# Block attention and a two-layer network on one core: the order list of the first two chunks written anew, and the intermediate tiles of the second layer moved to the front of on-chip memory

## The chip, the cores and the metric

The kernel runs on one core of a Trainium2 chip. Five engines work side by side, each through its own queue of instructions in program order: PE (matrix products), DVE (VectorE), ACT (ScalarE), POOL (GpSimd) and SP, which here issues the transfers (DMA). The metric is device time in microseconds (us): the median of the runs of the whole kernel, lower is better.

## The reference

```python
B, H, S, D = 4, 8, 768, 64;  block, window = 32, 16
k_sum = k.reshape(B, H, nb, block, D).max(axis=3)
v_sum = v.reshape(B, H, nb, block, D).mean(axis=3)
scores_l = where(|i - j| < window, scale * q @ k.T, -1e9)
scores_s = scale * q @ k_sum.T + log(block)
a = softmax(concat([scores_l, scores_s]))          # over the last axis
attn = a @ concat([v, v_sum])
x = attn.transpose(0, 2, 1, 3).reshape(3072, 512)
h = maximum(x @ w_in, 0)                           # w_in 512 x 2048
out = (h * h) @ w_out                              # w_out 2048 x 512
```

## The kernel before

Attention is worked in 24 tiles of 128 query rows (tile g). Two tiles make a chunk c of 256 rows of x, so there are twelve chunks. The network's weights are cut into 16 blocks f of 128 hidden units; block f holds both its part of w_in and its part of w_out. Each operand of a network product is split into a high and a low part, and each product is three matmuls (high by high, low weight by high, high by low): `ffn1` (line 403) is 12 matmuls of 256 columns for one f, `ffn2` (line 447) is 6 of 512 columns. xh and xl are the two parts of x (lines 387 and 390), gh and gl the two parts of the squared hidden values, w_sb the two parts of the weights. All weights stay on the chip once they are converted.

The weights come as 8-byte numbers into a room of 8192 bytes per partition (w_raw) and are turned into their parts by six steps: sign (ACT, line 239), round (ACT, line 246, or DVE, line 244), shift (DVE, line 250), add (POOL, line 255), copy of the high part into a second room (line 128) and subtraction that gives the low part (line 264, DVE or POOL). There are 18 rooms, so a late weight can only be loaded when an earlier w_raw room has been given back by its subtraction.

The loop over chunks 2 to 11 is regular: eight slots of two weight blocks for each chunk, with the attention of the next two tiles placed among them by `period`. Before it, the first two chunks, eight attention tiles and the conversion of all weights are worked in an order written out by hand, the string START. Each engine keeps that order for its own instructions. A token is a step, its indices, after them the engine (a, v, p for ACT, DVE, POOL) and after "=" the PSUM bank:

- `L:` a transfer on SP's queue (kv and kw: keys or values, transposed; q, k, v, x; w for weights; mask for the constants consts_sb); KS/KT and VT block maxima of keys and block sums of values (DVE, lines 190, 195); S scores; TT mask and row maximum of one head (DVE, line 307); SB and EX subtraction and exponential of four heads; NR, N the inverse of the sum and its product; T, TC turning by PE and copy out (line 128); TU turning by DVE (line 359); O outputs of a tile (line 373); XH, XL the parts of x.
- HI, LO, SH, AD, CA, SU the six steps of the conversion of weight f (`.0`, `.1`, `.2` mean whole, w_in half, w_out half).
- `F1.u.j`, `F2.u.j` first and second layer of unit u, half j. A unit is a pair of weight blocks for one chunk: units 0, 1 are pairs 0, 1 of chunk 0; 2 to 5 pairs 0 to 3 of chunk 1; 6 to 11 pairs 2 to 7 of chunk 0; 12 to 15 pairs 4 to 7 of chunk 1. RE, SQ, MU, GL make gh and gl from F1's result; EV moves a finished output out; Z are products with zeros while PE has nothing else.

The units named in ON_POOL have their gl made by POOL (line 654), the others by DVE (line 425):

```python
        elif op == "GL":
            gh, gl = flat(gh_sb, i % 2), flat(gl_sb, i % 2)
            if i in ON_POOL:
                nc.gpsimd.tensor_sub(out=gl, in0=r_of[i], in1=gh.bitcast(F32))
            else:
                low_square(gl, ph_of[i], gh)
```

Of the kernel before, what the change touches and what calls it, by code (L numbers as in the profile page):

```python
# [40 lines left out]


START = """
Z18 L:kv0 L:kv1 KS0 KS1 L:kv2 L:q0 L:kv3 L:q1 KS2 S0.0=01 Z3 S1.0=23 L:mask KS3 S1.1=23 PK4v L:w0.1 TT0.3 TT0.0 TT0.1
TT0.2 TT1.2 L:q2 XT PK5a SB0.0p S0.1=45 Z1 L:w1.1 TT1.3 L:w2.2 L:q4 TT1.0 LO0.1a L:q3 S2.0=01 S2.1=01 Z5 TT1.1 TT1.6
EX0.0 TT0.4 SB1.0p TT0.7 L:x1 HI0.1 TT0.6 TT0.5 EX1.0 NR0.0 SB0.1p TT1.5 EX0.1 HI1.1 L:x0 N0.0p TT1.7 HI2.2 T0.0=4 Z2
TT1.4 NR1.0 S3.1=52 NR0.1 SB1.1p TT2.0 SH1.1 S3.0=52 N0.1v TC0.0a TT2.3 TT2.1 N1.0p EX1.1 NR1.1 T0.1=3 L:x3 SH0.1
LO1.1a LO2.2a T1.0=4 TT2.7 TC0.1a CA0.1a CA1.1a TT2.6 SV0 L:x2 N1.1p TT2.5 TT2.2 SB2.0p TT3.3 TT3.0 T1.1=3 Z8 TT2.4
TT3.2 L:w2.1 TC1.0a TT3.1 L:k4 SB2.1v L:w1.2 L:w3.1 EX2.0 TT3.7 TC1.1a NR2.0 EX2.1 SV1 L:w4 SB3.0p TT3.4 N2.0p EX3.0
TT3.6 S4.1=01 TT3.5 HI2.1 L:q6 VC0.0a SB3.1p VC0.1a NR2.1 NR3.0 VC0.2v AD0.1 L:w0.2 VC1.3v VC1.2v L:k5 S4.0=01 T2.0=4  # L50
VC0.3a VC1.0v L:q5 N2.1p O0=3 EX3.1 VC1.1a NR3.1 N3.0p VX2a XH0 TC2.0v O1=2 T2.1=5 TT4.1 LO2.1a XL0 XH1 TC2.1v N3.1p
TT4.3 XL1 SU0.1p TT4.4 T3.0=4 TT4.5 L:w3.2 HI3.1 TT4.6 T3.1=3 TT4.7 LO1.2a O2=5 VX3a XH2 AD1.1 TC3.0a HI0.2 SU1.1v
F1.0.0=2 SH2.1 SH3.1 F1.0.1 TC3.1v TT4.2 S5.1=43 TT4.0 CA2.1a SH0.2 AD2.1 SU2.1v LO3.1a LO0.2a XL2 AD3.1 CA3.1a O3=0
SH2.2 HI1.2 L:w6 SU3.1v L:w7 S5.0=43 SH1.2 L:w5 XH3 LO3.2a TT5.0 RE0a XL3 F1.1.0=1 AD2.2 F1.1.1 SQ0 F1.3.0=5 MU0
F1.2.0=0 RE1v AD1.2 F1.2.1 AD0.2 F1.3.1 GL0v HI4 TT5.7 HI3.2 L:w11 CA0.2v L:w10 SH3.2 SU0.2v CA1.2a LO4a SH4 CA2.2a
SU1.2v CA3.2a CA4a SU2.2v SQ1 RE2v F2.0.0 LO5a L:w13 AD3.2 F2.0.1 MU1 SQ2 AD4 HI5 GL1v RE3a F2.1.0 MU2 SU3.2v HI6 L:w9
L:w8 F2.1.1 SU4v SH5 AD5 GL2v L:w14 EV0.1v EV0.0v LO6a SH6 CA5a SQ3 TT5.2 LO7v MU3 AD6 HI7 F1.6.0=2 F1.4.0=1 CA6a HI8
F2.2.0 GL3v LO9a F2.2.1 F2.3.0 LO8a F2.3.1 SU5v SU6v TT5.6 SH8 L:kw2 L:q7 SH7 F1.4.1 HI9 RE4v VT2 F1.6.1 TT5.4 CA7a
AD7 SQ4 E4.2 L:kw1 CA8a F1.5.0=0 E4.6 E5.2 MU4 AD8 L:k6 E4.4 F1.7.0=5 GL4v E4.7 TT5.1 TT5.3 F2.4.0 TT5.5 SU7v SU8v
LO10v F2.4.1 SH9 KT2 AD9 E4.3 F1.5.1 RE6v F1.12.0=1 E5.0 F1.7.1 LO11a CA9a SU9v RE5a HI10 L:w12 MU5 SQ5 HI12 HI11 SH10  # L60
GL5v MU6 HI13 F1.8.0=3 LO12a RE7v F1.8.1 SH12 AD10 CA10v SQ6 SU10v F1.12.1 E4.0 F2.5.0 E5.7 F2.5.1 F1.9.0=4 SH11 AD11
LO13a MU7 L:v4 F1.13.0=0 GL6v EV1.0a EV1.1a SQ7 VT1 CA12a GL7v RE8a AD12 E4.5 SU12v CA11a F2.6.0 SH13 CA13a E5.3 E4.1
E5.6 F2.6.1 SQ8 SU11v F2.7.0 NR4.1 L:kw3 F2.7.1 AD13 E5.5 HI14 LO14a F1.9.1 MU8 KT1 F1.10.0=2 SH14 NR4.0 L:k7 CA14a
SU13v GL8p RE9a E5.4 AD14 NR5.1 KT3 MU9 SQ9 F2.8.0 GL9v F1.14.0=5 SU14p L:w15 F2.8.1 N4.0v VT3 N4.1v E5.1 F1.10.1 HI15
RE10a SH15 F1.14.1 LO15a F1.11.0=3 MU10 CA15a AD15 F1.15.0=4 TU4.2 F2.9.0 F1.13.1 F2.9.1 SU15v F1.11.1 SQ10 L:kw0
TU4.1 GL10p NR5.0 RE11a F1.15.1 MU11 F2.10.0 KT0 SQ11 RE12v GL11p RE13a PK7a F2.10.1 S7.0=23 PK6v F2.11.0 L:v5 F2.11.1
SQ12 MU12 N5.1p GL12v TU4.0 EV2.1v EV2.0v S7.1=23 MU13 O4=1 SQ13 GL13p XH4 F2.12.0 RE14v N5.0p MU14 XL4 F2.12.1 TU5.2
S6.0=01 F2.13.0 RE15a S6.1=01 MU15 SQ14 F2.13.1 GL14p TU5.1 F2.14.0 F2.14.1 TU5.0 VT0 SQ15 O5=5 XH5 XL5 GL15p
"""


# [693 lines left out]
```

## Time and profile before

| what | value |
|---|---|
| time, median of 3 runs | 623.57 us (623.14 to 623.59) |
| the profiled execution, its own time | 622.91 us |
| its span, first to last instruction | 621.0 us |
| PE busy | 608.9 us, 98% of the span |
| DVE, ACT, POOL busy | 391.0, 266.8, 106.0 us |
| first F1 starts | 32.78 us after the span's start |
| last of the first two chunks, first F1 of chunk 2 | about 131 us |

Times below are in us from the start of the span, of the one profiled execution. "Idle before" in brackets is how long the engine had nothing to do before the row, with what ended it.

### The profile page before, as it was taken

Reading aid. Unit: us, or ns where it says so; the run is one execution under the profiler, and the core shown is the slowest. Engines: PE = TensorE matmul, PEld = TensorE weight load, DVE = VectorE, ACT = ScalarE, POOL = GpSimd, SP = SyncE. Lnnn points to the kernel's source line nnn. Section 1 sums busy time; section 2 is a strip of 40 time slices with the busy share of each in tenths; the row PEclk is TensorE's granted clock in tenths of the full one; section 3 lists DMA queues with packets and bytes.
Section 4 is the critical chain, followed back from the end, with each engine's and each line's share of the span. In section 5 each row is a group of like instructions: output and inputs, shape, how many; then the busy total and the mean of one; then the engine's idle time right before and its main releaser. Section 6 shows DMA issues by size and latency. Waiting matters only on the chain.

```text
span 621.0 us, 12930 instructions
## 1 busy us (share of the span) xinstructions
PE 608.9 (98%) x5253; PEld 546.3 (88%) x5253; DVE 391.0 (63%) x1054; ACT 266.8 (43%) x646; POOL 106.0 (17%) x103
## 2 busy tenths in 40 slices
...
PEclk9999999999999999999999999999999999999999
...
DMA packets 21643, 59.41 MB, mean 96 GB/s; under 512 B 2256, under 2 KB 2256, under 8 KB 20048
## 3 DMA queue, kind: packets, MB, share of 16 engines
...
## 4 chain that ended last, share of the span: by engine, by line
PE 83%; DVE 7%; ACT 4%; DMA 3%; issue 1%; POOL 1%; SPq 0%; ACTq 0%; DVEq 0%
PE o_ps L447 39%; PE ph L403 37%; PE ph L373 3%; PE s_ps L279 3%; DVE w_sb L264 2%; DMA w_raw<-in_w 2%; DMA consts_sb<-in_consts 1%; ACT w_raw L239 1%; PE s_ps L403 1%; DVE w_raw L250 1%; DVE e_sb L307 1%; ACT w_raw L246 1%; ACT xh L387 1%; DVE gl L425 0%; POOL e_sb L322 0%
## 5 line engine op out<-in xcount | busy, mean ns | idle before, releaser
L403 PE MATMUL ph<-xh,w_sb 128*128 128x256 f32 x1360 | 246.7, 282 | 1.2 <-ACT xh L387 0.7
L447 PE MATMUL o_ps<-w_sb,gh 128*128 128x512 f32 x768 | 239.2, 393 | 0.0
L403 PEld LDWEIGHTS ph<-xh,w_sb 128*128 128x128 f32 x1360 | 213.2, 188 | 8.9 <-issue 1.3
L403 PE MATMUL ph<-xl,w_sb 128*128 128x256 f32 x680 | 190.7, 280 | 0.2 <-DVE xl L390 0.2
L447 PEld LDWEIGHTS o_ps<-w_sb,gh 128*128 128x128 f32 x768 | 137.8, 188 | 25.7 <-issue 0.5
L422 DVE TENSOR_TENSOR ph<-ph,r 128x512 f32<-128x512 f32 x83 | 58.1, 699 | 151.8 <-ACT r L411 151.1
L447 PE MATMUL o_ps<-w_sb,gl 128*128 128x512 f32 x384 | 151.3, 394 | 0.3 <-DVE gl L425 0.3
L411 ACT ACTIVATE r<-ph 128x512 f32<-128x512 f32 x83 | 49.3, 594 | 200.8 <-PE ph L403 199.8
L403 PEld LDWEIGHTS ph<-xl,w_sb 128*128 128x128 f32 x680 | 128.7, 189 | 0.4 <-DVE xl L390 0.4
L359 DVE STREAM_TRANSPOSE pT<-e_sb 32x256 f32<-32x256 f32 x240 | 104.6, 436 | 5.2 <-POOL e_sb L346 1.9
L346 POOL TENSOR_TENSOR e_sb<-e_sb,total 128x480 f32<-128x480 f32 x45 | 44.1, 989 | 317.9 <-DVE total L340 176.3
L315 ACT ACTIVATE e_sb<-e_sb,nmx 128x120 f32<-128x120 f32 x160 | 61.4, 385 | 65.2 <-DVE nmx L307 65.2
L447 PEld LDWEIGHTS o_ps<-w_sb,gl 128*128 128x128 f32 x384 | 72.2, 188 | 16.4 <-DVE gl L425 1.1
L425 DVE TENSOR_TENSOR gl<-ph,gh 128x512 fp32r<-128x512 f32 x83 | 57.4, 692 | 8.6
L417 ACT ACTIVATE gh<-r 128x512 fp32r<-128x512 f32 x91 | 57.5, 632 | 4.2 <-PE o_ps L447 1.3
L307 DVE CUSTOM_DVE_ANT_0 e_sb<-s_ps,consts_sb 128x120 f32<-128x120 f32 x180 | 40.5, 277 | 0.9 <-DMA consts_sb<-in_consts 0.5
L255 POOL TENSOR_TENSOR w_raw<-w_raw 128x1024 int32<-128x1024 int32 (+1 forms) x20 | 33.5, 1680 | 36.4 <-DVE w_raw L250 25.6
L403 PE MATMUL s_ps<-xh,w_sb 128*128 128x256 f32 x176 | 32.4, 283 | 1.0 <-DVE w_sb L264 1.0
L315 ACT ACTIVATION_READ_ACCUMULATOR e_sb<-e_sb,nmx 128x1 f32 x160 | 30.0, 187 | 0.0
L403 PEld LDWEIGHTS s_ps<-xh,w_sb 128*128 128x128 f32 x176 | 27.4, 188 | 2.1 <-DVE w_sb L264 1.4
L390 DVE TENSOR_TENSOR xl<-ph,xh 128x512 fp32r<-128x512 f32 x20 | 13.8, 691 | 24.4 <-ACT xh L387 24.4
L403 PE MATMUL s_ps<-xl,w_sb 128*128 128x256 f32 x88 | 24.7, 281 | 0.0
...
## 6 DMA issues: line engine op xcount, KB each, us to landing
...
```

Of the source, the lines that this page charges most:

```text
L255: nc.gpsimd.tensor_tensor(out=lo, in0=hi, in1=lo, op=ALU.add)
L279: nc.tensor.matmul(s_ps[g, p // 2][r][ss, p, 0:NK], lhsT=q_sb[g % 3][rs, s, p, :], rhs=k_sb[g % 2][rs, :, s, p, :], start=True, stop=True,)
L307: nc.vector.tensor_tensor_reduce(out=e_sb(g)[:, h, 0:NK], in0=s_ps[g, half][h % 2][:, h // 2, 0:NK], in1=m, scale=-scale, scalar=3.0e38, o ...
L315: nc.scalar.activation(e, e, AF.Exp, bias=nmx[g, half][:, i : i + 1], scale=-1.0, accum_out=sm[g, half][:, i, 0:1])
L346: eng.tensor_mul(out=e, in0=e, in1=sm.pop((g, half)).unsqueeze(2).to_broadcast([P, 4, NK]))
L359: nc.vector.transpose(out=pT[g % 2][j * 32 : j * 32 + 32, :, i * 32 : i * 32 + 32], in_=e_sb(g)[i * 32 : i * 32 + 32, :, j * 32 : j * 32 + ...
L403: nc.tensor.matmul(ph, lhsT=w_sb[f][:, w, cc * P : (cc + 1) * P], rhs=x[c][:, cc, :], start=(n == 0), stop=(n == 3 * NC4 - 1))
L411: nc.scalar.activation(r, ph, AF.Relu)
L417: nc.scalar.activation(gh, r, AF.Square)
L422: nc.vector.tensor_mul(out=ph, in0=ph, in1=r)
L425: nc.vector.tensor_sub(out=gl, in0=ph, in1=gh.bitcast(F32))
L447: nc.tensor.matmul(o_ps[c][tt], lhsT=g_[:, ts_], rhs=w_sb[f][:, w, DM:], start=(first and n == 0), stop=(last and n == 2),)
```

## The change

Three things are changed.

START is a new string with the same steps, save that 29 products with zeros stand where 37 stood, and that some steps have another engine. `L:w2.1` comes early, w8, w12, k6 and the values' transfers come at other places, the last weight to be loaded is w14 instead of w15, and the subtraction (SU) of w8 and w9 is on POOL where that of w14 was.

ON_POOL is shorter: gl of the units 8, 10, 11 and 13 goes from POOL to DVE, that of unit 12 from DVE to POOL.

gh and gl lie in front of the constants, with 32 floats ahead of them; the gap behind is 16 floats instead of 56, and nmx has seven buffers instead of six. By the sizes, w_sb and w_raw begin at byte 56640 of a partition instead of 56896 (a room is 8192 bytes), xh at 204544 instead of 204768, xl at 212736 instead of 212960, gh at 1280 instead of 48128, gl at 5376 instead of 52224.

```diff
-ON_POOL = (8, 10, 11, 13, 14, 15, )
+ON_POOL = (12, 14, 15, )
...
-Z18 L:kv0 L:kv1 KS0 KS1 L:kv2 L:q0 L:kv3 L:q1 KS2 S0.0=01 Z3 S1.0=23 L:mask KS3 S1.1=23 PK4v L:w0.1 TT0.3 TT0.0 TT0.1
...
-S6.0=01 F2.13.0 RE15a S6.1=01 MU15 SQ14 F2.13.1 GL14p TU5.1 F2.14.0 F2.14.1 TU5.0 VT0 SQ15 O5=5 XH5 XL5 GL15p
+Z18 L:kv2 XT KS2 L:kv0 L:kv1 L:kv3 KS0 L:q0 L:mask KS1 KS3 PK5v L:q1 S0.0=01 S0.1=23 TT0.2 TT0.3 TT0.1 TT0.0 TT0.7
...
+RE15a F2.12.0 F2.12.1 SQ14 F2.13.0 MU15 F2.13.1 O4=4 TU5.1 SQ15 GL14p GL15p S7.1=23 F2.14.0 S7.0=23 O5=5 XH4 F2.14.1
+XH5 XL4 XL5
...
     w_sb = {}
+    const.tile([P, 32], F32, name="gap0")
+    gh_sb = const.tile([P, 4, CT], F32R, name="gh")
+    gl_sb = const.tile([P, 4, CT], F32R, name="gl")
     consts_sb = const.tile([P, 3 * NK + P + 8 * 32], F32, name="consts_sb")
...
-    const.tile([P, 56], F32, name="gap0")
-    gh_sb = const.tile([P, 4, CT], F32R, name="gh")
-    gl_sb = const.tile([P, 4, CT], F32R, name="gl")
-
     sm_sb = const.tile([P, 8, 4, 2], F32, name="sm")
...
-    const.tile([P, 56], F32, name="gap")
+    const.tile([P, 16], F32, name="gap")
...
-            nmx[g, half] = work.tile([P, 4], F32, name="nmx", tag="nmx", bufs=6)
+            nmx[g, half] = work.tile([P, 4], F32, name="nmx", tag="nmx", bufs=7)
```

On SP's queue at the very start of the program, before the change (kv are the transposed keys of the first batch, 768 columns each):

```order
1 L182 DMA kv<-in_kt 128x768 x3
2 L132 DMA q_sb_75<-in_q 128x512
3 L182 DMA kv<-in_kt 128x768
4 L132 DMA q_sb_76<-in_q 128x512
5 L566 DMA consts_sb<-in_consts 128x744
6 L228 DMA w_raw<-in_w 128x512
```

and with the change:

```order
1 L182 DMA kv<-in_kt 128x768 x4
2 L132 DMA q_sb_78<-in_q 128x512
3 L566 DMA consts_sb<-in_consts 128x744
4 L132 DMA q_sb_79<-in_q 128x512
5 L132 DMA q_sb_80<-in_q 128x512
6 L228 DMA w_raw<-in_w 128x512 x2
```

The constants with the mask now stand ahead of the second q instead of behind it, and the fourth kv ahead of the first q.

On SP's queue, the last transfers of the list, before (w_raw_1052 is w12, w_raw_1274 is w15):

```order
41 L228 DMA w_raw_1052<-in_w 128x1024
42 L142 DMA v_sb0_73<-in_v 96x2x512
43 L186 DMA kv_1197<-in_kt 128x768
44 L187 DMA kv_1197<-in_vt 128x768
45 L135 DMA k_sb1_72<-in_k 128x768
46 L228 DMA w_raw_1274<-in_w 128x1024
47 L186 DMA kv_1385<-in_kt 128x768
```

and with the change (w_raw_1015 is w15, 1019 w10, 1078 w13, 1157 w14):

```order
41 L228 DMA w_raw_1015<-in_w 128x1024
42 L228 DMA w_raw_1019<-in_w 128x1024
43 L228 DMA w_raw_1078<-in_w 128x1024
44 L186 DMA kv_1085<-in_kt 128x768
45 L187 DMA kv_1085<-in_vt 128x768
46 L135 DMA k_sb1_75<-in_k 128x768
47 L132 DMA q_sb1_79<-in_q 128x512
48 L228 DMA w_raw_1157<-in_w 128x1024
```

w15 has moved ahead of w10, w13 and w14, and the last weight is w14. Its room is the one that w10 gives back; before, that of w15 was the one that w13 gave back.

On PE, the end of the list and the first F1 of chunk 2, before (row 476 is O5):

```order
474 L447 MATMUL o_ps<-w_sb,gh 128x512 x2
475 L447 MATMUL o_ps<-w_sb,gl 128x512
476 L373 MATMUL ph<-pT_81,v_sb_74 64x64 x16
477 L403 MATMUL ph<-xh,w_sb 128x256 x2
478 L403 MATMUL ph<-xl,w_sb 128x256
```

and with the change (row 435 is O5, rows 436 to 439 are F2.14.1):

```order
434 L279 MATMUL s_ps<-k_sb_75,q_sb_79 64x120 x8
435 L373 MATMUL ph<-pT_84,v_sb_77 64x64 x16
436 L447 MATMUL o_ps<-w_sb,gh 128x512 x2
437 L447 MATMUL o_ps<-w_sb,gl 128x512
438 L447 MATMUL o_ps<-w_sb,gh 128x512 x2
439 L447 MATMUL o_ps<-w_sb,gl 128x512
440 L403 MATMUL ph<-xh,w_sb 128x256 x2
441 L403 MATMUL ph<-xl,w_sb 128x256
```

Six matmuls of the second layer now stand between the last outputs of chunk 2's x and the first matmul that reads that x.

## Rows read from the trace of the kernel before

**Rows 1.** The page: busy time of the engines (share of the span, instructions), and the granted clock of PE in 40 slices, 9 being full speed.

```profile
PE 608.9 (98%) x5253; PEld 546.3 (88%) x5253; DVE 391.0 (63%) x1054; ACT 266.8 (43%) x646; POOL 106.0 (17%) x103
...
PEclk9999999999999999999999999999999999999999
```

**Rows 2.** Busy time by stretch: stretch and its length, then PE, PEld (weight loads of PE), DVE, ACT, POOL busy with their instructions, the granted clock, DMA share, GB/s.

```profile
32.78:131.50 98.72, 96.31 (x761) 84.64 (x758) 88.64 (x154) 65.84 (x110) 44.34 (x27) 1.00 0.48 178
131.50:621.00 489.50, 485.33 (x3978) 439.79 (x3978) 277.63 (x792) 181.31 (x502) 40.45 (x45) 1.00 0.19 61
...
10.00:20.00 10.00, 8.47 (x259) 7.00 (x252) 9.38 (x53) 7.39 (x14) 6.12 (x7) 1.00 1.03 404
```

**Rows 3.** What PE waited for from 32.5 to 132 us: engine, tile and line that waited, what it waited for, total us, times, longest.

```profile
PE s_ps L403 <- DVE w_sb L264: 1.0, 1, 1.0
PE ph L403 <- ACT xh L387: 0.7, 1, 0.7
PE o_ps L447 <- DVE gl L425: 0.3, 1, 0.3
...
```

**Rows 4.** The chain that ended last (start, length, what): the outputs of two tiles, with which each chunk of the regular loop ends, two of them one chunk apart, and between them one slot's second layer and the next slot's first.

```profile
170.79 2.02 PE ph L373 x64
...
177.62 2.75 PE o_ps L447 x12
180.37 2.85 PE ph L403 x24
...
219.62 2.02 PE ph L373 x64
```

**Rows 5.** PE's timeline in the regular loop, the first and the last xl matmul of two first-layer slots (24 matmuls each; start, length). The first two rows belong to the slot behind the scores, the others to the next slot.

```profile
223.70 0.28 PE L403 MATMUL ph<-xl,w_sb 128*128 128x256 f32 x1
...
226.16 0.28 PE L403 MATMUL ph<-xl,w_sb 128*128 128x256 f32 x1
...
229.27 0.28 PE L403 MATMUL ph<-xl,w_sb 128*128 128x256 f32 x1
...
231.76 0.28 PE L403 MATMUL ph<-xl,w_sb 128*128 128x256 f32 x1
```

**Rows 6.** The start of the program: a piece of the chain (the mask's transfer), three of DVE's rows that waited, the last xl of chunk 0, and PE's O2 and first F1.

```profile
3.52 7.02 DMA consts_sb<-in_consts
...
10.72 0.28 DVE L307 CUSTOM_DVE_ANT_0 e_sb<-s_ps,consts_sb 128x120 f32<-128x120 f32 x1 [0.48 <-DMA consts_sb<-in_consts]
...
29.86 0.69 DVE L390 TENSOR_TENSOR xl<-s_ps,xh 128x512 fp32r<-128x512 f32 x1 [0.42 <-ACT xh L387]
30.87 0.69 DVE L128 COPY pT<-ph 128x512 f32<-128x512 f32 x1 [0.31 <-PE ph L352]
...
31.67 0.69 DVE L390 TENSOR_TENSOR xl<-s_ps,xh 128x512 fp32r<-128x512 f32 x1
...
31.70 1.15 PE L373 MATMUL ph<-pT,v_x 128*64 128x64 f32 x32
32.78 0.51 PE L403 MATMUL s_ps<-xh,w_sb 128*128 128x256 f32 x2
```

**Rows 7.** DVE's timeline: the shift of two half weights.

```profile
16.44 1.26 DVE L250 TENSOR_SCALAR w_raw<-w_raw 128x512 int32<-128x512 int32 x1
...
19.36 0.40 DVE L250 TENSOR_SCALAR w_raw<-w_raw 128x512 int32<-128x512 int32 x1
```

**Rows 8.** The late weights, from the timelines of DVE, SP's queue, PE, ACT and POOL: the subtraction of w13, the issue of w15, F1.10.1 (the first reader of w13), and the sign, add and subtraction of w15.

```profile
93.06 2.92 DVE L264 TENSOR_TENSOR w_sb<-w_raw,w_sb 128x1024 fp32r<-128x1024 f32 x1
...
96.04 0.33 SPq L228 DMA_DIRECT2D w_raw<-in_w  x1
...
96.62 0.40 PE L403 MATMUL s_ps<-xh,w_sb 128*128 128x256 f32 x2
...
100.79 1.15 ACT L239 ACTIVATE w_raw<-w_raw 128x1024 f32<-128x1024 f32 x1 [4.97 <-DVE e_sb L346]
...
103.53 1.89 POOL L255 TENSOR_TENSOR w_raw<-w_raw 128x1024 int32<-128x1024 int32 x1 [5.25 <-ACT w_raw L246]
...
105.46 2.29 DVE L264 TENSOR_TENSOR w_sb<-w_raw,w_sb 128x1024 fp32r<-128x1024 f32 x1 [0.37 <-POOL w_raw L255]
```

**Rows 9.** PE's timeline at the end of the list: O5 and the first F1 of chunk 2.

```profile
128.96 1.15 PE L373 MATMUL ph<-pT,v_sb 128*64 128x64 f32 x32
130.79 0.51 PE L403 MATMUL ph<-xh,w_sb 128*128 128x256 f32 x2 [0.68 <-ACT xh L387]
131.52 0.39 PE L403 MATMUL ph<-xl,w_sb 128*128 128x256 f32 x1 [0.22 <-DVE xl L390]
```

**Rows 10.** Groups of DVE and POOL from 32 to 131.5 us (count, busy, mean ns of one, idle before): DVE's subtraction, its block maxima of keys and its gl; POOL's gl and its one subtraction. Then one row of DVE's timeline.

```profile
L264 DVE TENSOR_TENSOR w_sb<-w_raw,w_sb 128x1024 fp32r<-128x1024 f32 (+1 forms) x18 | 22.6, 1276 | 1.0 <-POOL w_raw L255 0.9
L425 DVE TENSOR_TENSOR gl<-s_ps,gh 128x512 fp32r<-128x512 f32 x7 | 4.8, 686 | 0.9 <-ACT gh L417 0.7
L190 DVE TENSOR_REDUCE ksum<-kv 128x24 f32<-128x768 f32 x4 | 3.8, 940 | 0.0
...
L654 POOL TENSOR_TENSOR gl<-r,gh 128x512 fp32r<-128x512 f32 x6 | 7.8, 1296 | 15.3 <-ACT gh L642 14.4 <-DVE r L648 0.9
L264 POOL TENSOR_TENSOR w_sb<-w_raw,w_sb 128x1024 fp32r<-128x1024 f32 x1 | 3.3, 3309 | 0.1
...
90.18 0.69 DVE L648 TENSOR_TENSOR r<-s_ps,r 128x512 f32<-128x512 f32 x1 [1.53 <-ACT gh L417]
```

More of the change, by code (lines that the diff above doesn't have):

```diff
@@ L43 @@
 START = """
-Z18 L:kv0 L:kv1 KS0 KS1 L:kv2 L:q0 L:kv3 L:q1 KS2 S0.0=01 Z3 S1.0=23 L:mask KS3 S1.1=23 PK4v L:w0.1 TT0.3 TT0.0 TT0.1
[L45 to L67, printed above, removed]
-S6.0=01 F2.13.0 RE15a S6.1=01 MU15 SQ14 F2.13.1 GL14p TU5.1 F2.14.0 F2.14.1 TU5.0 VT0 SQ15 O5=5 XH5 XL5 GL15p
+Z18 L:kv2 XT KS2 L:kv0 L:kv1 L:kv3 KS0 L:q0 L:mask KS1 KS3 PK5v L:q1 S0.0=01 S0.1=23 TT0.2 TT0.3 TT0.1 TT0.0 TT0.7
@@ new lines @@
+S1.1=45 TT0.5 SB0.0p TT0.4 TT0.6 EX0.0 SB0.1p TT1.6 PK4a L:q2 TT1.5 S2.0=01 Z1 L:w2.1 L:w1.1 TT1.7 EX0.1 L:q3 L:w0.1
+HI1.1 TT1.4 SB1.1p NR0.0 S1.0=45 NR0.1 L:k4 EX1.1 N0.0p LO2.1a TT1.2 N0.1p L:x1 S2.1=01 Z2 TT1.1 TT1.3 T0.0=2 Z1
+T0.1=3 Z1 LO0.1a TT1.0 HI2.1 NR1.1 SB1.0v SH1.1 TT2.0 S3.0=45 L:q4 TT2.1 S3.1=45 N1.1p TT2.2 EX1.0 TT2.6 TC0.0a L:x0
+L:x2 TT2.3 SB2.0p NR1.0 TT2.4 TC0.1a HI0.1 N1.0p EX2.0 T1.1=2 Z4 CA1.1a T1.0=3 LO1.1a L:x3 TT2.5 L:w3.1 TT2.7 TT3.6
+TT3.5 TT3.7 SH0.1 SH2.1 SB2.1p TT3.4 S4.0=01 CA0.1a TC1.1a NR2.0 SB3.1v SV0 Z2 N2.0p TT3.1 EX2.1 L:w1.2 TT3.3 SV1
@@ new lines @@
+TC1.0a EX3.1 VC0.2a L:w3.2 TT3.2 L:q5 TT3.0 VC0.1a SB3.0p T2.0=2 NR2.1 S4.1=01 N2.1p VC0.0v VC0.3a VC1.2a VC1.1v EX3.0
+NR3.1 HI3.1 O0=4 AD0.1 VC1.0v VC1.3v N3.1p XH0 VX2a NR3.0 T2.1=5 O1=3 TC2.1v L:w0.2 XH1 CA2.1a L:k5 N3.0p T3.1=5
+TC2.0v VX3a XL0 XL1 SU0.1p AD2.1 TT4.2 LO3.1a AD1.1 T3.0=2 O2=4 TC3.0v L:w8 LO3.2a F1.0.0=3 XH2 L:w4 HI0.2 TC3.1v
+SU2.1v SH3.1 O3=2 SU1.1v CA3.1a XH3 F1.1.0=5 XL2 HI3.2 TT4.7 AD3.1 LO0.2a F1.0.1 L:w2.2 SU3.1v SH0.2 HI1.2 CA0.2a
+HI2.2 TT4.6 XL3 LO2.2a L:w6 AD0.2 F1.1.1 SH3.2 F1.2.0=4 L:w7 SU0.2v RE0a SQ0 SH1.2 CA3.2a SH2.2 LO1.2a TT4.0 L:w5
@@ new lines @@
+F1.2.1 L:k6 HI4 MU0 GL0v TT4.1 CA2.2a L:kw3 TT4.3 RE1a AD3.2 L:kw2 TT4.5 RE2v CA1.2a AD2.2 AD1.2 F1.3.0=2 TT4.4 SH4
+CA4v SU2.2v L:v4 LO4a F1.3.1 SQ1 SU1.2v HI6 MU1 S5.0=30 GL1v S5.1=30 F2.0.0 MU2 F2.0.1 AD4 F2.1.0 SU3.2v SU4v SQ2 SH6
+HI5 F2.1.1 L:w12 RE3a L:kw0 LO5a EV0.0a LO7a SH5 LO6a GL2v L:w11 HI8 F1.6.0=1 E4.6 EV0.1v KT3 CA5v F1.4.0=5 F2.2.0 SQ3
+AD5 SU5v MU3 F2.2.1 AD6 CA6a F1.4.1 F1.6.1 GL3v HI7 SU6v LO8a F2.3.0 F1.5.0=4 SH7 CA7a L:w9 L:v5 SH8 RE4v SQ4 AD7 VT2
+SU7v HI9 LO9a AD8 KT2 CA8a F2.3.1 HI11 LO11a F1.7.0=2 F1.5.1 MU4 E4.5 GL4v RE5v SQ5 F1.7.1 F2.4.0 SU8p F2.4.1 TT5.0
```

8 lines of the change are left out of this document (added).

## The prediction

> **What bounds the kernel now.** I read the page first. PE is busy for 608.9 of 621.0 us and its granted clock is 9 tenths or more, 2.4 GHz, in every slice [rows 1]. So only two things can shorten the kernel: time in which PE waits, and the pace of its matmuls. The stretches come next [rows 2]. From the first F1 at 32.78 to 131.5 us, where the list ends, PE is busy for 96.31 of 98.72 us: 2.41 us are left to gain there. From 131.5 to the end it is busy for 485.33 of 489.50, and the chain is all PE. In the regular loop the outputs of two tiles start at 170.79 and again at 219.62 [rows 4], so a chunk takes 48.83 us; the diff leaves that order alone. Ahead of 32.78 the network has not begun, and the length of this start counts in full. The waits name the 2.41 us [rows 3]: 1.0 for a weight's low part (DVE line 264), 0.7 for xh, 0.3 for gl; another 0.22 for xl stands in the rows at the end of the list [rows 9]. Four questions follow: when F1 starts, what becomes of these waits, whether new ones appear, and whether the new places change PE's pace.
>
> **The change, part by part.**
>
> *The start.* The mask's transfer ends at 3.52 + 7.02 = 10.54, and DVE's first mask and maximum starts at 10.72, having been idle for 0.48 [rows 6]. DVE was thus ready at 10.24. On SP's queue the mask now passes the second q, of 128 x 512 x 4 bytes = 262 KB, and the last kv passes the first q. At 404 GB/s, the rate from 10 to 20 us [rows 2], 262 KB are 0.65 us. The mask and DVE's last key maxima both come earlier by that, so neither holds back the other: -0.65. From there to the last xl of chunk 0, which starts at 31.67, and to F1 at 32.78 [rows 6] DVE is the engine with the most work, and both lists give it nearly the same steps. I therefore keep the rest at nothing. The bounds: two of its idle times there, 0.42 and 0.31 [rows 6], may close, which makes -1.4; or one more half-weight shift takes 1.26 instead of 0.40 us, as one of the two did [rows 7], which eats the gain and makes +0.2.
>
> *The last weight.* w15 is issued at 96.04, when w13's subtraction (93.06, 2.92 us) has given back the room, and its own subtraction ends at 105.46 + 2.29 = 107.75 [rows 8]. That is 11.7 us for transfer and conversion, and PE waits 1.0 for it [rows 3]. In the new list w15 is loaded earlier, and the last weight is w14, in the room that w10's subtraction gives back. That subtraction must be done before F1.9.0 can run. Between F1.9.0 and the first use of w14, F1.11.0, the new list has seven halves of F1 and five of F2 on PE. A slot's two F1 halves are 2.85 us and two F2 halves 2.75 [rows 4], so this is 7 x 1.425 + 5 x 1.375 = 16.9 us of work to hide a chain of 11.7. The wait goes: -1.0 (0 if something else holds w14).
>
> *The end of the list.* O5 starts at 128.96; the first F1 of chunk 2 waits 0.68 for xh and then 0.22 for xl [rows 9]. F2.14.1 now stands between the two: six matmuls, 1.375 us, as above. xl of tile 4 can be made before. After O5 come xh and xl of tile 5, 0.90 us beyond what PE needs without a pause; 1.375 covers it. -0.90. Bounds: -0.90 and 0.
>
> *New load on DVE.* Counted along the two lists ahead of the subtraction of w13 (SU13), DVE gets two key maxima and two value sums of the second batch (0.94 each), six steps of 128 x 512 (0.69 each; gl of units 8 and 9 among them), a rounding, a shift and two high copies (about 0.7 each). It loses the subtractions of w8 and w9 (1.28 each), three such 128 x 512 steps and five small ones, about 2.3 us together. By the means of the groups [rows 10] that is 10.7 against 6.9, or 3.8 to 4.4 more by how the small steps are priced. I take 4.2. F1.10.1, which reads w13, stands 1.4 us of PE work later, so DVE has 2.8 us less room. Before, SU13 ended at 95.98 and F1.10.1 started at 96.62 [rows 8], 0.64 us of room; 2.8 - 0.64 = 2.2 us late if all that DVE lost ahead of it comes back. Two losses stand there: 1.53 idle for gh [rows 10], and 1.64 because the subtraction took 2.92 instead of its mean 1.28 [rows 8, 10], beside a subtraction of 3.31 on POOL. More queued work fills the idle time, since DVE then arrives later than gh. Of the long subtraction I cannot say so. 2.2 - 1.53 = 0.7: I take +0.7, with the bounds 0 (neither comes back) and +2.2 (both do).
>
> The trace shows two shifts of one shape at 1.26 and 0.40 us [rows 7], and two subtractions at 2.92 and the mean 1.28. The Trainium skill, "SBUF — State Buffer", section "Who interferes with whom", has a rule for that: a VectorE instruction with two inputs in SBUF contends with a GpSimd instruction that reads SBUF, and 2-port modes block it for a whole instruction. The trace agrees as far as these rows go. By that rule two more subtractions on POOL (w8, w9) slow DVE's neighbours, while four fewer gl there free them; it speaks for the upper bound without giving a sum.
>
> *gl and the shorter ON_POOL.* POOL's gl takes 1.30, DVE's 0.69 [rows 10]. The unit's F2 can start 0.6 earlier, but F2 waited for gl only 0.3 us in the whole list [rows 3]. No gain; its work on DVE is counted above.
>
> *The places.* xh, xl and the weights move against one another by 32 bytes (xh 224 down, weights 256 down). What that does to PE no row shows: all first-layer matmuls of this run have one and the same offset modulo 512 bytes (rooms lie 8192 apart). A pace other than the usual one exists, though. Between the first and the last xl matmul of a slot are 21 steps: 2.49 / 21 = 118.6 ns in an ordinary slot, 2.46 / 21 = 117.1 in the slot behind the scores [rows 5], with the same operands' offset. There are 12 chunks x 16 blocks x 12 = 2304 such matmuls; seven slots in eight run at 118.6, so 2016 x 1.43 ns = 2.9 us would be won if all ran at 117.1. I take the nearest row for the bound on both sides: -2.9 and +2.9, and the value 0, since the two paces occur with one placement and so something else sets them.
>
> The Trainium skill, "TensorE: Matmul & The Clock Gate", section "Step-by-step: what each phase is for", says that loading the next weights does not steal SBUF read bandwidth from the running matmul, as each has its own read port. By that the placement is worth exactly 0, and the sum is the one below; but no run here has varied the placement, so the two cases with another pace keep a chance.
>
> **The sum.** -0.65 - 1.0 - 0.90 + 0.7 = -1.85 on the profiled execution's own 622.91 us, 1.9 more than its span. The median of the runs is 0.66 higher, 623.57. So 623.57 - 1.85 = 621.7 us. Anything under 0.2%, 1.25 us, is about what a measurement of this kernel cannot tell from no change: faster is below 622.32, slower above 624.82.
>
> **The rivals.**
>
> *A, the pace improves.* All first-layer slots go to 117.1 ns. For it: the lower pace occurs in this trace, so 118.6 is not a floor. Against it: it occurs without any other placement. 621.7 - 2.9 = 618.8.
>
> *B, the pace worsens* by as much: 621.7 + 2.9 = 624.6. The same rows speak for and against; nothing says which way an offset would work.
>
> *C, the other side: VectorE cannot convert w10 to w13 in time.* The new load of 2.8 us makes it late at F1.10.1 by 2.2, and if one or two subtractions ahead take 2.92 like w13's before, each adds 1.64: 2.2 + 1.64 to 3.28 = 3.8 to 5.5 of new waits on the weights instead of 0.7. 621.7 + 3.1 to 4.8 = 624.8 to 626.5, 625.6 in the middle. It decides for slower once DVE's lateness exceeds the gains by 1.25, that is 2.55 + 1.25 = 3.8 us. For it: DVE is busy for 88.64 of 98.72 us in this stretch [rows 2]. Against it: 10 us idle there, and SU13 did meet its time.
>
> *D, the list is only shuffled.* The 2.41 us of waits turn up elsewhere and the start stays bound by DVE at 32.8: 623.5. For it: the steps and PE's work are the same, and every wait now is small.
>
> **How the numbers follow.** The forecast 0.50 (its own range 620.3 to 623.0: the start at -1.4 or DVE at +2.2, the terms not both at their ends), A 0.17, B 0.07, C 0.13, D 0.13. Faster: 0.44 of the forecast and A's 0.17, 0.61. Same: 0.06 of the forecast, D's 0.12, and 0.04 of B, 0.22. Slower: C, 0.03 of B and 0.01 of D, 0.17. The range must leave out no more than 0.2: C (0.13), the far half of B and the lower tail of A. 618.2 to 624.7.
>
> **What would show it.** The start: first mask and maximum at about 10.1 instead of 10.72 and F1 at about 32.1. The last weight: the waits view without a wait of 1.0 for line 264 ahead of F1.11. The end: the first F1 of chunk 2 directly behind six line-447 matmuls, with no bracket. New load: a wait for line 264 at F1.10.1 of 0 to 2.2. The places: a chunk again 48.83 us long, 21 steps again in 2.49. The prediction is wrong if the chunk's period differs by more than 0.1 us, as ten chunks then carry 1 us or more, or if F1 starts later than 32.8.

## The result and the profile after

The changed kernel takes 613.41 us (median of 4 runs, 612.61 to 613.97) against 623.43 before: a ratio of 0.9839, with a 95% interval of 0.9822 to 0.9856. That is 10.0 us less, where 1.9 was forecast and the range ended at 618.2. Its profiled execution has a span of 612.0 us, 613.97 in all, and so lies at the upper end of its runs.

The page's first row, and the busy time by stretch (stretch, length, PE, PEld, DVE, ACT, POOL busy with their instructions, granted clock, DMA share, GB/s), cut at the first F1 and where chunk 2 begins:

```profile
PE 599.2 (98%) x5245; PEld 537.0 (88%) x5245; DVE 394.5 (64%) x1054; ACT 266.9 (44%) x647; POOL 106.2 (17%) x102
...
33.70:131.00 97.30, 95.10 (x760) 83.98 (x758) 91.17 (x161) 65.86 (x111) 44.54 (x27) 1.00 0.51 179
131.00:612.00 481.00, 476.81 (x3981) 432.17 (x3979) 277.47 (x792) 181.45 (x502) 40.48 (x45) 1.00 0.19 62
```

Against [rows 2] the list is 1.4 us shorter by these cuts, the start 0.9 longer, and the regular loop, whose order is the same, is 481.0 instead of 489.5. PE is as full as before and its clock is the same; it does the same matmuls in less time. The chain shows where:

```profile
169.53 2.02 PE ph L373 x64
...
176.28 2.75 PE o_ps L447 x12
179.03 2.75 PE ph L403 x24
...
217.49 2.02 PE ph L373 x64
```

Two outputs are 47.96 us apart, not 48.83 [rows 4], and a slot's first layer takes 2.75 instead of 2.85. The 12 matmuls of the second layer stay at 2.75. In PE's timeline, the first and last xl matmul of the slot behind the scores and of the next one:

```profile
221.58 0.28 PE L403 MATMUL ph<-xl,w_sb 128*128 128x256 f32 x1
...
223.97 0.28 PE L403 MATMUL ph<-xl,w_sb 128*128 128x256 f32 x1
...
227.06 0.28 PE L403 MATMUL ph<-xl,w_sb 128*128 128x256 f32 x1
...
229.46 0.28 PE L403 MATMUL ph<-xl,w_sb 128*128 128x256 f32 x1
```

21 steps are 2.39 and 2.40 us, 113.8 and 114.3 ns each, where [rows 5] gave 117.1 and 118.6. Seen one by one, the ordinary slot has five steps of 116 to 123 ns and then steady ones of 113, 113, 114 to its end; behind the scores only two or three steps come before them. Before, the steps were steady too, in another way: they came back every five matmuls, as 116, 117, 119, 122, 120 in the ordinary slot and as 115, 118, 117, 120, 117 behind the scores, each to the end of its slot.

The list behaved otherwise than forecast too. PE's waits from the first F1 to chunk 2, and the places of two of them:

```profile
PE s_ps L403 <- DVE w_sb L264: 1.4, 1, 1.4
PE ph L403 <- DVE w_sb L264: 0.6, 1, 0.6
...
59.71 0.39 PE L403 MATMUL ph<-xh,w_sb 128*128 128x256 f32 x1 [0.55 <-DVE w_sb L264]
...
91.14 0.39 PE L403 MATMUL s_ps<-xh,w_sb 128*128 128x256 f32 x1 [1.43 <-DVE w_sb L264]
...
88.17 2.92 DVE L264 TENSOR_TENSOR w_sb<-w_raw,w_sb 128x1024 fp32r<-128x1024 f32 x1
```

The waits of [rows 3] at F1.11 and at the list's end are gone, but the weights' low parts are waited for at two other places, at F1.4.1 (w5) and F1.9.1 (w11), 1.98 us together.

### The profile page after: what moved, and what is told of

Its sections match the earlier page's. It is cut to its first block, busy times and chain, and to the rows that moved or that the text cites. A ratio compares the mean times of both kernels' runs of the same rounds, so it can differ in the third digit from the quotient of the medians.

```text
span 612.0 us, 12926 instructions
## 1 busy us (share of the span) xinstructions
PE 599.2 (98%) x5245; PEld 537.0 (88%) x5245; DVE 394.5 (64%) x1054; ACT 266.9 (44%) x647; POOL 106.2 (17%) x102
## 4 chain that ended last, share of the span: by engine, by line
PE 85%; DVE 7%; DMA 6%; issue 1%; ACT 1%; SPq 0%; POOL 0%; DVEq 0%; POOLq 0%
PE o_ps L447 40%; PE ph L403 37%; DMA w_raw<-in_w 5%; PE ph L373 3%; PE s_ps L279 3%; DVE w_sb L264 2%; PE s_ps L403 1%; DVE w_raw L250 1%; DMA q_sb<-in_q 1%; DVE gl L425 1%; DVE ksum L190 0%; DVE ph L422 0%; DVE s_ps L422 0%; DVE r L413 0%; POOL w_raw L255 0%
## 5 line engine op out<-in xcount | busy, mean ns | idle before, releaser
L403 PEld LDWEIGHTS ph<-xh,w_sb 128*128 128x128 f32 x1408 | 218.4, 188 | 9.4 <-issue 1.3
L403 PE MATMUL ph<-xl,w_sb 128*128 128x256 f32 x704 | 195.0, 277 | 0.0
L422 DVE TENSOR_TENSOR ph<-ph,r 128x512 f32<-128x512 f32 x86 | 60.1, 699 | 143.7 <-ACT r L411 142.9
L403 PEld LDWEIGHTS ph<-xl,w_sb 128*128 128x128 f32 x704 | 132.4, 188 | 0.0
L346 POOL TENSOR_TENSOR e_sb<-e_sb,total 128x480 f32<-128x480 f32 x47 | 46.5, 999 | 319.2 <-DVE total L340 173.2
L425 DVE TENSOR_TENSOR gl<-ph,gh 128x512 fp32r<-128x512 f32 x86 | 59.5, 692 | 9.2 <-DVE ph L422 0.5
L390 DVE TENSOR_TENSOR xl<-ph,xh 128x512 fp32r<-128x512 f32 x22 | 15.2, 690 | 25.0 <-ACT xh L387 25.0
L264 DVE TENSOR_TENSOR w_sb<-w_raw,w_sb 128x1024 fp32r<-128x1024 f32 (+1 forms) x17 | 25.5, 1511 | 0.3
L387 ACT CAST xh<-ph 128x512 fp32r<-128x512 f32 x22 | 12.9, 586 | 28.9 <-PE ph L373 28.9
L403 PE MATMUL s_ps<-xh,w_sb 128*128 128x256 f32 x128 | 23.2, 281 | 1.4 <-DVE w_sb L264 1.4
```

What stands on the lines that cost most here:

```text
L264: eng.tensor_sub(out=w_[:, 1], in0=words(f, j)[0].bitcast(F32), in1=w_[:, 0].bitcast(F32))
L346: eng.tensor_mul(out=e, in0=e, in1=sm.pop((g, half)).unsqueeze(2).to_broadcast([P, 4, NK]))
L403: nc.tensor.matmul(ph, lhsT=w_sb[f][:, w, cc * P : (cc + 1) * P], rhs=x[c][:, cc, :], start=(n == 0), stop=(n == 3 * NC4 - 1))
L422: nc.vector.tensor_mul(out=ph, in0=ph, in1=r)
L425: nc.vector.tensor_sub(out=gl, in0=ph, in1=gh.bitcast(F32))
```

## The experiments

Distances below are those in bytes from the place of a weight room, modulo 512, by the tiles' addresses: x stands for xh and xl, g for gh and gl. Before: x 416, g 448. After: both 448. Paces are differences between the starts of neighbouring matmuls in the trace. The six kernels s1 to s4, p5 and p6 ran once each, so they are read by their traces and not by their times.

A chunk's slots need care. In the code the outputs and scores for the next chunk stand behind the slot of f = 12. The slot behind the scores is therefore the last of its chunk (f = 14 and 15) and still reads that chunk's x; the next chunk begins one slot later. In chunk 10 there are no scores: its last slot stands behind the outputs and a pause for xl.

### Which part of the change: four kernels

**p1_old_list_new_place**: START and ON_POOL of before, everything else of after.

> The order list and ON_POOL of before with the places of after. Theory P (the places alone make the first layer's matmuls faster): a chunk of the regular loop takes 47.96 us as in the changed kernel, ten chunks gain 8.7 and the list's 384 first-layer matmuls about 1.6, so about 613.1. Theory L (the new list makes the gain, by leaving the regular loop in another state): 48.83 a chunk and about 623.4.

**p2_new_list_old_place**: START and ON_POOL of after, everything else of before.

> The new order list and ON_POOL with the places of before. Theory P: a chunk takes 48.83 us; the start 0.9 longer, the end of the list 0.9 shorter, so about 623.4. Theory L: 47.96 a chunk and about 613.4.

**p3_nmx7_only**: one more 16-byte buffer (it takes 32 bytes) ahead of x.

```diff
-    const.tile([P, 56], F32, name="gap0")
+    const.tile([P, 48], F32, name="gap0")
...
-            nmx[g, half] = work.tile([P, 4], F32, name="nmx", tag="nmx", bufs=6)
+            nmx[g, half] = work.tile([P, 4], F32, name="nmx", tag="nmx", bufs=7)
```

> Before, with nmx of seven buffers and the first gap 8 floats shorter, so that xh and xl stay where they were and gh, gl and the weights come 32 bytes lower: x minus weights is 448 bytes modulo 512 instead of 416, gh minus weights 448 as ever. Theory D (the distance of x from the weights, modulo 512, sets the pace of the first layer): 47.96 a chunk, about 613.1. Theory A (it is where gh and gl lie, in front, or the absolute addresses): 48.83 a chunk, 623.4.

**p4_front_only**: START and ON_POOL of before, gh, gl and the gaps of after, nmx with six buffers.

> The order list of before, gh and gl in front and the gaps as in after, but nmx with six buffers: x minus weights stays at 416 bytes modulo 512 as in before. Theory D: 48.83 us a chunk and 623.4. Theory A: 47.96 and 613.1.

| kernel | list | x, g | us | ratio to before, interval |
|---|---|---|---|---|
| before | old | 416, 448 | 623.67 | 1 |
| p1 | old | 448, 448 | 615.03 | 0.9864 (0.9848 to 0.9881) |
| p2 | new | 416, 448 | 622.63 | 0.9988 (0.9978 to 0.9997) |
| p3 | old | 448, 448 | 614.59 | 0.9856 (0.9841 to 0.9871) |
| p4 | old | 416, 448 | 623.27 | 0.9996 (0.9987 to 1.0005) |

The places alone give 8.6 to 9.1 us, the new list alone 1.0, and the two together the 10.0. Moving gh and gl to the front does nothing (p4); the 32 bytes between x and the weights do it all (p3). In p3 g minus weights is -8768 bytes, in after -55360, alike only modulo 512, and a chunk takes 47.94 and 47.96 us; so for g neither the absolute place nor the whole distance counts. For x the whole distance is the same in both; s1 below compares that.

Theories P and D had 613.1 for p1 and p3, which lie 1.9 and 1.5 above it. From the first F1 to chunk 2 the list took 98.07 and 98.03 us, where before it took 98.01: its faster matmuls gained nothing there. In p1 chunk 2 stayed slow as well.

### Is it the distance of x alone? No

**s1_staggered**: each room of the weights 32 bytes longer, so that every weight block has another distance.

```diff
-        return big.tile([P, 8192 // mybir.dt.size(dtype)], dtype, name=name, tag="w", bufs=NF + SPARE)
+        return big.tile([P, 8224 // mybir.dt.size(dtype)], dtype, name=name, tag="w", bufs=NF + SPARE)[:, 0 : 8192 // mybir.dt.size(dtype)]
```

> Before, with every room of the weights 32 bytes longer, so that the sixteen weight blocks lie at fifteen different places modulo 512 bytes while xh, xl and gh, gl have one each (the two gaps are gone and total has three buffers, to make room). Theory D (the distance of the moving operand from the weights, modulo 512, sets the pace) expects that in the regular loop each block has a pace of its own, the same in every chunk: 118.6 ns per first-layer matmul at x minus weights = 416, about 114 at 448, and something between or beyond at the others. Theory B (it is a matter of all operands at once, or of chance) expects one pace for all blocks. The time as a whole lies between 613 and 640 us and decides nothing.

625.86 us. The blocks differ, in the same way in all chunks: the last ten steps of a block are 114.9 to 120.1 ns on the mean. The fastest block is f = 13, the one that stands at 448. It is the second in the last slot ahead of the outputs, behind f = 12 at 352. The first and the last xl matmul of both blocks, and the outputs:

```profile
215.05 0.28 PE L401 MATMUL ph<-xl,w_sb 128*128 128x256 f32 x1
...
216.13 0.28 PE L401 MATMUL ph<-xl,w_sb 128*128 128x256 f32 x1
...
216.48 0.29 PE L401 MATMUL ph<-xl,w_sb 128*128 128x256 f32 x1
...
217.51 0.28 PE L401 MATMUL ph<-xl,w_sb 128*128 128x256 f32 x1
...
220.52 2.09 PE L371 MATMUL ph<-pT,v_sb 128*64 128x64 f32 x64
```

Nine steps are 1.08 us in f = 12, 120.0 ns, and 1.03 in f = 13, 114.4; one by one f = 13 has four steps of 114 to 123 and then 113, 113, 114 to its end. The blocks at 0, 320 and 480 have 120.0, 117.8 and 118.4, within 0.1 of what s2 finds for these places; others, with eleven steps to settle in, are up to 1.4 off. f = 12 and f = 15 stand 257 x 512 bytes apart, both at 352, and have 119.7 and 120.1: distances alike only modulo 512 gave like paces. So this run speaks for theory D. The expectation of s2, which says that the block at 448 kept 118.7 and that 113 to 114 came at 352, counts the slots from the scores on and so is one slot off.

**s2_chunk_places**: one distance for all blocks, but another in each chunk; g at 448 throughout.

```diff
-            x[c] = work.tile([P, NPAIR, CT], F32R, name=name, tag=name)
+            wide = work.tile([P, NPAIR * CT + 72], F32R, name=name, tag=name)
+            at = (PLACE[c] - (288 if c % 2 else 0) - (64 if name == "xl" else 0)) // 4 if c > 1 else 0
+            x[c] = wide[:, at : at + NPAIR * CT].rearrange("p (n t) -> p n t", n=NPAIR)
```

> Before, with xh and xl of each chunk of the regular loop at a distance of its own from the weights (x minus weights modulo 512: 0 in chunk 2, then 256, 32, 320, 64, 352, 128, 384, 192 and 480 in chunk 11), the weights and gh at one place (gh minus weights 448 as ever); the mean's constants lie in r to make room. The staggered run did not bear theory D out: its block at 448 kept 118.7 ns, and only the second half of one slot (352) came to 113 to 114 ns after six matmuls. Theory D' (the distance decides, but only if it holds over a whole slot) expects the same pace in all eight slots of a chunk and other paces in other chunks, some of them 114. Theory G (what counts is gh against x, or where x stands by itself) expects paces that do not go by this distance alone; told apart by the next run.

624.65 us. First-layer pace in ns behind second-layer slots, the same in all slots of a chunk: x at 0 and 256: 120.0; 32: 117.0; 64, 192, 320: 117.8; 128, 384: 119.9; 352: 119.6; 480: 118.3; with 416 (118.6, before) and 448 (114.3, after) that is twelve of sixteen places, and one alone is fast. The other four stand in s1 alone, in one block each, at 116.9 to 119.5. But chunk 10, at 192, came to 113.3 ns in its last slot, though nothing in the addresses changed:

```profile
565.94 0.51 PE L406 MATMUL ph<-xh,w_sb 128*128 128x256 f32 x2 [0.48 <-DVE xl L393]
```

This slot began behind the outputs and a pause, the seven before it, at 117.8, each behind a second layer. At 128 and 384 the slot behind the scores has 118.8 instead of 119.9.

**p5_nmx7_gh_stays**: as p3, but the gap behind gh and gl is cut instead of the one ahead of them: x 448, g 480.

> As p3 (x minus weights 448), but gh and gl stay where they were before, so gh minus weights is 480 instead of 448, and x minus gh 480 as in before instead of 0. Theory D' expects the first layer at 114 ns a matmul as in p3, and at most the second layer's pace changed; a chunk 48 us if that is unchanged. Theory G (x against gh) expects the first layer at 118.6.

624.59 us: the gain is gone, although x stands at 448. So the distance of x alone does not decide, and theories D and D' fall here. The chain of p5, a slot behind the scores and the next one, and of both slots a stretch of PE's timeline:

```profile
224.00 2.94 PE ph L403 x24
226.94 2.80 PE o_ps L447 x12
229.74 2.83 PE ph L403 x24
232.57 2.80 PE o_ps L447 x12
...
224.62 0.28 PE L403 MATMUL ph<-xl,w_sb 128*128 128x256 f32 x1
...
226.66 0.28 PE L403 MATMUL ph<-xl,w_sb 128*128 128x256 f32 x1
...
230.16 0.28 PE L403 MATMUL ph<-xl,w_sb 128*128 128x256 f32 x1
...
232.28 0.28 PE L403 MATMUL ph<-xl,w_sb 128*128 128x256 f32 x1
```

18 steps are 2.04 us in the first, 113.3 ns, and 2.12 in the second, 117.8. Same operands' places, same work, two paces. All eight slots behind the scores came to 113.3. What differs is what PE did just before: scores in the one case, the second layer, itself slower at 2.80, in the other.

p1 shows the same without any odd place. Its chain in chunk 2 and in chunk 3:

```profile
153.98 2.83 PE ph L402 x24
156.81 2.77 PE o_ps L446 x12
...
180.26 2.75 PE ph L402 x24
183.01 2.75 PE o_ps L446 x12
```

x and g stand at 448 in both chunks. Chunk 2 was entered behind a pause for xh and xl and stayed at 2.83 and 2.77 in its slots up to the next scores; from those scores on all slots take 2.75. In p3 chunk 2 had nearly the same pause (steps of 504 and 222 ns, in p1 505 and 227) and took 2.75 at once. What of the entry decides is not shown. In after, with F2.14.1 ahead of it, chunk 2 runs at 2.75 from the start, but the last slot of chunk 10, behind outputs and a pause, has 117.8.

### How the layers hand over

**s3_gh_places**: x at 448 in all chunks, g at another place in each.

```diff
-    gh_sb = const.tile([P, 4, CT], F32R, name="gh")
-    gl_sb = const.tile([P, 4, CT], F32R, name="gl")
+    wide = [const.tile([P, 4 * CT + 128], F32R, name=n) for n in ("gh", "gl")]
+
+    def placed(c):
+        o = (PLACE.get(c, 448) - 448) % 512 // 4
+        return [t_[:, o : o + 4 * CT].rearrange("p (a b) -> p a b", a=4) for t_ in wide]
```

> Before, with xh, xl at 448 from the weights (modulo 512) in all chunks, as in the changed kernel, and gh, gl at a distance of its own in each chunk of the regular loop (gh minus weights 416 in chunk 2, then 384, 352, 320, 256, 192, 128, 64, 32 and 0 in chunk 11); the mean's constants lie in r to make room. The runs so far: in the run with one x distance for each chunk and gh at 448 no distance but 448 gave 113 ns behind a second-layer slot; with x at 448 and gh at 480 only the slot behind the scores came to 113, the seven behind a second-layer slot stayed at 118. Theory E (the first layer has several steady patterns, and how it is entered from the second layer, whose pattern hangs on gh minus weights, picks the one): the slot behind the scores at 113 in most chunks, the other slots at 113 in some chunks and at 117 to 120 in others. Theory D' (x against the weights alone): 113 everywhere, against the run with gh at 480. Theory G (x must equal gh modulo 512): 113 nowhere, the slot behind the scores included.

619.40 us. The slots behind the scores came to 113 in all chunks but one; the others as theory E had it. They are told here by the place of the g that the second layer just ahead reads. With g at 416 or 32 all are at 113 to 114 after a few matmuls, with g at 352, 256 and 0 all stay at 117.8, and with 384, 320, 128 and 64 they alternate. With g at 192 five stay at 117.8, and the two that follow the slot behind the scores have 113.3: there both patterns go on as they began. The chain in chunk 3 (g at 384), and in chunk 6 (256):

```profile
196.63 2.73 PE ph L409 x24
199.36 2.77 PE o_ps L454 x12
202.13 2.83 PE ph L409 x24
204.96 2.78 PE o_ps L454 x12
...
342.45 2.83 PE ph L409 x24
345.28 2.72 PE o_ps L454 x12
```

The first layer thus has two steady patterns at x = 448, 113.3 and 117.8 ns, and the way it is entered picks one. The second layer has a better pattern too, 2.72, but with that the first layer settles at 2.83: 5.55 for the slot against 5.50 in after.

**p6_both_480**: nmx with eight buffers and both gaps 8 floats shorter: x 480, g 480.

> Before, with x and gh both at 480 from the weights, so x minus gh is 0 as in the changed kernel, but neither at 448. Theory G (x must equal gh): 113 ns in all slots, a chunk about 48 us. Theory E expects no such thing of equality: the slots behind the second layer at 117 to 120 as with gh at 480 before, a chunk 48.7 to 49.1 us, unless 480 happens to enter well.

626.14 us, the first layer at 118.2 ns, a chunk 49.13 us. That x and g are equal is no rule; theory G falls.

**s4_x_places_gh0**: as s2, with the gap such that g stands at 0.

> Before, with gh, gl at 0 from the weights (modulo 512), where the run over gh's places showed the fastest second layer (226.6 ns a matmul instead of 229.0) but the first layer at 117.8 for x at 448, and xh, xl at a distance of its own in each chunk (480 in chunk 2, then 256, 0, 320, 32, 352, 64, 384, 192 and 416 in chunk 11). Theory E (x's and gh's distances together pick the pattern): the second layer at 226.6 only where the first layer leaves it in the right state, the first layer at 117 to 120 in most chunks; one at 113 together with 226.6 would give slots of 5.44 us instead of 5.49. Theory D' (each layer by its own distance): the second layer at 226.6 in all chunks, the first layer in each chunk as in the run with gh at 448 (120.0 at 0, 117.0 at 32, 119.6 at 352 and so on).

622.64 us. The first layer's paces are within 0.7 ns of those with g at 448: 120.0 at 0 and 256, 116.7 at 32, 117.8 to 117.9 at 64, 192 and 320, 120.3 at 352, 119.9 at 384, 118.1 at 480, and 119.0 at 416. So behind a second-layer slot x alone fixes the first layer at these places, as theory D' says; g mattered at x = 448 alone. At 192 the last slot of chunk 10 came to 113.3 here too. The second layer came to its best pattern throughout only with x at 192 (226.7). None of these gives a slot under 5.50. In s3 two single slots took 5.46 and 5.47 us, with 113 to 114 ns and a second layer at 228, and the next ones 5.55; of all that lasted, 448 and 448 has the shortest slot.

### What the new list is bound by

**b1_swap**: after, with F2.7.1 and F1.9.1 exchanged in START.

> The changed kernel with F2.7.1 ahead of F1.9.1 instead of behind it. In the changed kernel F1.9.1 waits 1.43 us for the subtraction of w11, which took 2.92 us. If that wait is what the new list's load on VectorE costs, six matmuls of 1.375 us hide it: about 1.2 to 1.4 us less than the changed kernel, 612.1. If the wait only turns up at the next weight (F1.10.0 or F1.10.1), no change: 613.4.

613.39 us, 0.9835 (0.9822 to 0.9848): no change. F1.9.1 no longer waits; ten microseconds later F1.10.1 does, for the next weight but one:

```profile
100.45 0.39 PE L403 MATMUL s_ps<-xh,w_sb 128*128 128x256 f32 x1 [0.95 <-DVE w_sb L264]
```

**b2_less_dve**: after, with four steps moved from DVE to ACT in START.

```diff
-RE5v ... EV1.0v ... LO10v ... LO14v
+RE5a ... EV1.0a ... LO10a ... LO14a
```

> The changed kernel with four steps of its list moved from VectorE to ScalarE: the relu of unit 5, the eviction of chunk 1's first half-sum (EV1.0), and the rounding of w10 and w14. Moving F2.7.1 ahead of F1.9.1 had only moved the wait of 1.43 us to F1.10.1 (0.95, and 0.3 at a second-layer matmul). Theory V (VectorE, busy for 38.97 of the 40 us from 60 to 100, is the bound there, by sheer work): the four steps are about 2.8 us of its work, so the waits of 1.43 and 0.55 shrink to some 0.5 together and the time falls by about 1.0 to 1.4, to 612.2. Theory W (it is the one subtraction of 2.92 us beside POOL's add, wherever it stands): the wait of 1.43 stays, 613.4.

611.43 us, 0.9813 (0.9794 to 0.9832): 2.0 less than the changed kernel by the medians, and the fastest of all; one of its five runs, 613.67, lies among those of the changed kernel. PE's waits in its list, the stretch from 60 to 100 us in b2 and then in after, the subtractions of w11 and w14 in b2, and there the first F1 of chunk 2:

```profile
PE ph L403 <- DVE w_sb L264: 0.5, 1, 0.5
...
PE o_ps L447 <- DVE w_sb L264: 0.2, 1, 0.2
PE s_ps L403 <- DVE w_sb L264: 0.2, 1, 0.2
...
60.00:100.00 40.00, 39.84 (x267) 36.23 (x267) 38.22 (x63) 35.21 (x58) 21.70 (x11) 1.00 0.44 161
...
60.00:100.00 40.00, 38.35 (x254) 34.47 (x254) 38.97 (x64) 31.95 (x55) 22.19 (x10) 1.00 0.48 166
...
86.90 1.22 DVE L264 TENSOR_TENSOR w_sb<-w_raw,w_sb 128x1024 fp32r<-128x1024 f32 x1
...
99.25 2.92 DVE L264 TENSOR_TENSOR w_sb<-w_raw,w_sb 128x1024 fp32r<-128x1024 f32 x1
...
128.59 0.40 PE L403 MATMUL ph<-xh,w_sb 128*128 128x256 f32 x2
```

VectorE was busy for 38.97 of 40 us in after, and PE lost 1.65. With less work on VectorE PE loses 0.16, and chunk 2 begins 2.3 us earlier, 0.2 of it from the start. Theory W falls as it was put: a subtraction of 2.92 us stands in this list too, that of w14, and PE did not lose 1.43 by it. Theory V had the direction right, but it is not shown that sheer work is the bound. VectorE is still busy for 38.22 us, and the subtraction of w11 took 1.22 instead of 2.92: with 2.92 it would have ended at 89.82, 1.3 us after F1.9.1 began at 88.52. So at w11 the wait went because the long subtraction moved to a weight that PE needs later (F1.11.0 begins at 102.66); this run does not separate that from the smaller load. From the first F1 to chunk 2 are 95.11 us instead of 97.22; 1.3 of these 2.1 are waits that went, and 0.5 is a first layer that ran at 116.9 instead of 118.3 ns on the mean of the list's 384 matmuls, for a reason that was not traced.

## Why the prediction was wrong

**The places: the step that failed.** I took 0, with 2.9 us as the bound on both sides, and it measured 8.6 to 9.1 (p1, p3). The observation was right: two paces occur at one placement [rows 5]. The conclusion was not: "so something else sets them" left out that a placement can decide which of several patterns is reached, and that the reachable ones may lie below both paces of the trace. The pattern at 113.3 did not occur in the regular loop of before. 117.1 was the other steady pattern of the placement of before, in the slot behind the scores. It tells what another entry gives at that placement, and it bounds nothing for another placement. The Trainium skill, "TensorE: Matmul & The Clock Gate", section "Step-by-step: what each phase is for", gives each of the two streams a read port of its own and says that weight loads steal nothing from a running matmul; the pace that followed 32 bytes does not agree with the sum of 0 that I drew from it. Rival A had the right kind and a third of the size. The sign that the forecast named was the right one: the chunk's period differs by 0.87 us, far beyond 0.1. What inside PE makes one placement faster stays open.

**The start: half right.** The first mask and maximum came at 9.74 (forecast 10.1, before 10.72), but F1 at 33.70 instead of 32.1, also later than the 32.8 that the forecast named as a sign of being wrong:

```profile
9.74 0.28 DVE L307 CUSTOM_DVE_ANT_0 e_sb<-s_ps,consts_sb 128x120 f32<-128x120 f32 x1 [0.47 <-PE s_ps L295]
...
16.23 1.21 DVE L250 TENSOR_SCALAR w_raw<-w_raw 128x512 int32<-128x512 int32 x1
...
20.75 1.59 DVE L250 TENSOR_SCALAR w_raw<-w_raw 128x512 int32<-128x512 int32 x2
...
26.21 0.42 DVE L128 COPY v_sb<-o_ps 32x256 f32<-32x256 f32 x1 [0.76 <-ACT v_sb L128]
27.45 0.42 DVE L128 COPY v_sb<-o_ps 32x256 f32<-32x256 f32 x1 [0.82 <-ACT v_sb L128]
...
33.70 0.50 PE L403 MATMUL s_ps<-xh,w_sb 128*128 128x256 f32 x2
```

"Both lists give it nearly the same steps" was wrong: the new list has three half-weight shifts ahead of F1 where the old had two, 2.80 us against 1.66 [rows 7], because w2.1 comes early, and VectorE waits 0.76 and 0.82 for ScalarE's part of the value means. How much of the 0.9 is the list stays open: the old list's F1 began at 32.78, 32.77, 33.26 and 33.81 in the profiles of before, p1, p3 and p4, the new one's at 33.70, 33.17, 33.40 and 33.48 in after, p2, b1 and b2. The forecast gain is in none of them.

**The last weight and the end: right.** No F1.11 waits for w14 or w15. The first F1 of chunk 2 starts directly behind six matmuls of the second layer and without a bracket, where [rows 9] had 0.68 and 0.22:

```profile
128.34 1.15 PE L373 MATMUL ph<-pT,v_sb 128*64 128x64 f32 x32
129.42 0.73 PE L447 MATMUL o_ps<-w_sb,gh 128*128 128x512 f32 x2
...
130.92 0.40 PE L403 MATMUL ph<-xh,w_sb 128*128 128x256 f32 x2
```

**New load on VectorE: right in kind, too small.** +0.7 at F1.10.1 became 1.43 at F1.9.1, two weights earlier (w11), and 0.55 at F1.4.1 (w5), for which the forecast had no term: 1.98 together, inside the bounds of 0 to 2.2. b1 shows that the place is not fixed: where PE does not wait at w11, it waits at w13. The long subtraction came back, the idle time did not, as assumed. Its neighbour was misread, though: before, POOL's subtraction began when VectorE's had 1.0 us left, and what ran beside it till then was POOL's add, as at w11 now:

```profile
93.00 1.90 POOL L255 TENSOR_TENSOR w_raw<-w_raw 128x1024 int32<-128x1024 int32 x1 [0.69 <-ACT w_raw L246]
94.98 3.31 POOL L264 TENSOR_TENSOR w_sb<-w_raw,w_sb 128x1024 fp32r<-128x1024 f32 x1
```

Moreover the faster first layer also reaches each weight sooner, which I had not counted. p1 shows it: with the old list and the new pace PE waited 1.7 us for w_sb and 0.9 for gl in the list, against 1.0 and 0.3 before, and the list took as long as before.

**The sum.** For the list and ON_POOL alone the forecast was -1.85, and p2 measured -1.0, about half. The 10.0 us of the result are for the most part the term that the sum had at 0.
